# A planned attention kernel: heads paired four apart in eight q transfers, weights in 1 KB runs, a new order

## The chip, the cores and the metric

The kernel runs on one core of a Trainium2 chip. Five engines work side by side, each with its own instruction queue that it follows in order: PE (TensorE) multiplies and transposes into PSUM, DVE (VectorE) and ACT (ScalarE) copy from PSUM and compute elementwise, POOL (GpSimd) computes on SBUF, SP (SyncE) issues transfers, as ACT does in the beginning. The metric is the device time of one execution in microseconds (us), the median of several runs.

## The reference

Eight batches of 8 heads, 576 tokens, 64 channels. The first part is linear attention without a softmax, then a root-mean-square norm for each head; the second part is a mixture of four causal attention heads of which each token takes two.

```
kv  = einsum('bhsd,bhse->bhde', k, v)
out = einsum('bhsd,bhde->bhse', q, kv)
x   = out / sqrt(mean(out*out, -1) + 1e-6) * g_norm     # heads side by side: (8, 576, 512)
top-2 of x @ w_gate, softmax over the two              # gate of each token
for each of 4 experts: a = causal softmax(q k^T / 8) with q, k, v = x @ wq, wk, wv
    result += gate * (a @ v @ wo)
```

## The kernel before, in words

Tokens go in five blocks of 128 (the last has 64); the 512 channels go in four chunks of 128, a chunk being a pair of heads. Steps have short names, and the same names stand in the list that is planned:

- `lk`, `lv`, `lkr`, `lvr`, `lq` load k, v (512 tokens, then the remaining 64) and q; `lg0`, `lw`, `lwo` load the norm's weights, the gate, wq, wk, wv and wo. All go through SP, those of batch 0 half through ACT.
- `kv` multiplies k and v on PE, for each chunk two heads in the two halves of PSUM; `kvx` and `kvc` copy it; `kt`, `kg` fold the gate's weights in, so that `out` (q times kv) gives 64 channels and 4 gate values for each head.
- q must have channels on partitions. In batch 0 PE transposes it (`q`, `qc`); in the others it is loaded in 32-token pieces and DVE transposes blocks of 32 (L523).
- `oc` copies out, `sq` and `red` make the mean square, `nw` are eleven small Newton steps, `gl` to `gate` make the gates on DVE (`sh` is a subtraction, L660), `xm` scales x on POOL (L635), `x` transposes it on PE (L514), `xc` copies it.
- `v`, `qp`, `kp` project, `sc`, `exp`, `msk`, `pv` are the causal attention, `oc2`, `ot`, `y` its output, `yc` the copy of y into one of four buffers, `st` the store on SP.

The order of all instructions is written out when the program is built. `graph` lists the steps with an engine, assumed times, what each needs and which buffers it uses; `plan` walks through a model of the engines and takes the step of least `urgency` among those that can start first. The result is a fixed order on each engine; the times in those tables are the planner's assumptions. PSUM has two small buffers (`sm`) and three large ones (`bg`). DMA completions use eight semaphores in turn, so a transfer can wait for one issued eight earlier.

Of the kernel before, what the change touches and what calls it, by code (L numbers as in the profile page):

```python
# [17 lines left out]
QPE = 1  # L18
# [4 lines left out]
LOADS = ("lk", "lv", "lkr", "lvr", "lq", "lg0", "lw", "lwo", "st")  # L23


def graph(B):
    t = {}
# [16 lines left out]
    R5, R4, R2 = range(NB), range(NCH), range(EP)
    for b in range(B):

        q2 = "ACT" if b == 0 else "SP"
        for p in R4 if b == 0 else R2:
            w = 1.0 if b == 0 else 2.0
            old = [("kv", b - 2, c) for c in R4] if p == 0 else []  # L50
            add(("lk", b, p), "SP", 0.5, 0.5 * w, old, (("k", b),))
            add(("lv", b, p), q2, 0.5, 0.5 * w, old, (("v", b),))
        add(("lkr", b), "SP", 0.6, 0.7, [("kv", b - 2, c) for c in R4])
        add(("lvr", b), q2, 0.6, 0.7, [("kv", b - 2, c) for c in R4])
        for i in R5 if b < QPE else R4:
            add(("lq", b, i), q2 if i % 2 else "SP", *((0.7, 1.35 if i < NF else 0.7) if b < QPE else (2.2, 2.1)), [], (("q", b),))
        if b == 0:
            add(("lg0",), "ACT", 3.8, 0.2)
            dve(("wg",), 0.45, [("lg0",)])
            for nm in "qkv":  # L60
                for p in R2:
                    add(("lw", nm, p), "SP", 1.0, 1.5, (), (("x", nm, p),))
                    dve(("ws", nm, p), 0.48, [("lw", nm, p), ("lg0",)], (("x", nm, p),))
            for p in R2:
                add(("lwo", "o", p), "SP", 0.5, 1.5, (), (("y", "wo", p),))
                dve(("wo", "o", p), 0.42, [("lwo", "o", p)], (("y", "wo", p),))

        for c in R4:
            piece = c if b == 0 else c // 2
            pe(("kv", b, c), 0.82, [("lk", b, piece), ("lv", b, piece), ("lkr", b), ("lvr", b)], (("sm", "kv", b), ("k", b), ("v", b)))  # L70
        dve(("kvx", b), 0.84, [("kv", b, c) for c in R4] + [("out", b - 2, i) for i in R5], (("sm", "kv", b),))
        act(("kvc", b), 0.37, [("kvx", b), ("kt", b - 2)], (("sm", "kv", b),))
        for i in R5:
            if b < QPE:
                last = i == NF
                pe(("q", b, i), 0.38 if last else 0.44, [("lq", b, i)], (("sm", "q", b, i), ("q", b)))
                dve(
                    ("qc", b, i), 0.42 if last else 0.69, [("q", b, i), ("out", b - 1, i), ("out", b - 1, NF)],
                    (("sm", "q", b, i),),
                )  # L80
# [4 lines left out]
        pe(("kg", b), 0.45, [("ktc", b), ("wg",)], (("sm", "kg", b), ("kvT", b)))
        dve(("kgc", b), 0.34, [("kg", b)] + [("out", b - 2, i) for i in R5], (("sm", "kg", b),))
        for i in R5:
# [4 lines left out]
            dve(  # L92
                ("oc", b, i), 0.73, [("out", b, i), ("xm", b - 1, i), ("gl", b - 1), ("sq", b - 1, i)],
# [66 lines left out]
NF = 4  # L160
POOLS = {
# [4 lines left out]
PERIOD = 25.8  # L166
URGENCY = {
    "den": (-64.6, 21.14, -2.99), "ex": (43.8, 42.17, -5.95), "exp": (-101.9, 8.59, 2.67),
# [3 lines left out]
    "ktc": (-437.7, -29.37, 14.27), "kv": (-44.1, 6.07, 24.1), "kvc": (-223.2, 5.31, 24.45),  # L172
# [703 lines left out]
```

## Time and profile before

| | |
|---|---|
| median of 3 runs | 276.47 us (275.64 to 278.58) |
| profiled execution | 276.96 us, its span 275.2 us |
| PE busy | 229.5 us (83%) |
| DVE, ACT, POOL busy | 178.8, 157.7, 77.0 us |
| mean granted clock of PE | 0.919 |
| transfers | 40.28 MB, 146 GB/s over the span |

Busy time is a mean over stages of different kind; a stage is read from its own stretch. In a timeline row the first number is the start in us, the second the duration; in brackets stands the idle time before it and what ended it. SPq and ACTq are the issue of transfers. The granted clock is 1.00 or 0.50 at any time; means of a stretch lie between.

### The profile page before, as it was taken

The numbers are of one execution on the slowest core, as the hardware profiler recorded it, in microseconds if no ns is written. First come the engines' busy times: TensorE is split into PE (matmuls) and PEld (weight loads), VectorE is DVE, ScalarE is ACT, GpSimd is POOL, SyncE is SP. The second block draws the span as 40 slices with busy tenths as digits, with TensorE's granted clock in tenths as the row PEclk, the third lists the DMA queues.
The fourth block names the chain that finished last, engine by engine and source line by source line (L and its number), as shares of the span: only waits on it lengthen the run. The fifth ranks groups of instructions, "written<-read, shape, count | busy, mean of one in ns | idle before, by whom it ended". The sixth has DMA issues, their size and how long they took to land.

```text
span 275.2 us, 6438 instructions
## 1 busy us (share of the span) xinstructions
PE 229.5 (83%) x2423; PEld 204.3 (74%) x2436; DVE 178.8 (65%) x501; ACT 157.7 (57%) x282; POOL 77.0 (28%) x154
## 2 busy tenths in 40 slices
PE   1359387999999969995199799999499999999982
PEld 1358375999999859984179789889498989888950
DVE  0537885399889799837016855689978977712540
ACT  0020313278664837792257757369259679899773
POOL 8100061004800632360002821006601801912320
PEclk9986855699999999999569979999979999999999
DMA  7999989999589789689977931220003104005035
GB/s 233 236 163 268 220 151 262 221 168 283 85 184 271 119 192 250 114 244 226 239 156 186 227 102 23 74 79 0 2 1 136 38 2 173 2 0 175 1 136 210
DMA packets 109039, 40.28 MB, mean 146 GB/s; under 512 B 87760, under 2 KB 104144, under 8 KB 109008
## 3 DMA queue, kind: packets, MB, share of 16 engines
q1 hardware_dynamic: 104576, 38.16, 60.1%
q10 hardware_dynamic: 4432, 1.71, 2.9%
q8 instruction: 19, 0.31, 0.5%
q14 instruction: 12, 0.10, 0.1%
HBM read 30.42 MB, written 9.44 MB: 145 GB/s over the span
## 4 chain that ended last, share of the span: by engine, by line
PE 55%; DVE 15%; SPq 10%; DMA 7%; ACT 5%; issue 4%; ACTq 1%; POOL 0%; DVEq 0%; POOLq 0%
PE p_out L560 8%; PE p_sc L739 7%; PE p_v L695 7%; PE p_q L713 6%; PE p_k L713 6%; SPq L447 6%; PE p_x L514 5%; PE p_kv L496 5%; PE p_pv L773 4%; PE p_y L821 4%; DMA v_b<-in_v_dram 3%; DMA g_wide<-in_g_norm_dram 2%; DVE inv L794 2%; DMA out_dram<-y 2%; SPq L473 2%
## 5 line engine op out<-in xcount | busy, mean ns | idle before, releaser
L759 POOL TENSOR_SCALAR_AFFINE_SELECT PT<-PT 128x256 bf16<-128x256 bf16 (+1 forms) x80 | 29.7, 387 | 145.9 <-ACT PT L753 141.3
L753 ACT ACTIVATE PT<-p_sc 128x576 bf16<-128x576 f32 (+3 forms) x80 | 52.3, 717 | 7.8 <-PE p_sc L739 7.5
L635 POOL TENSOR_TENSOR x_tok<-o_sb,rs 128x512 f32<-128x512 f32 (+1 forms) x40 | 41.5, 1053 | 40.1 <-DMA q_b<-in_q_dram 29.0
L560 PE MATMUL p_out<-kvx,qT 128*128 128x136 f32 x320 | 44.7, 292 | 0.5 <-DVE osc L801 0.4
L576 ACT ACTIVATE sq<-o_sb 128x512 f32<-128x512 f32 (+1 forms) x40 | 25.4, 641 | 32.8 <-DVE o_sb L570 24.4
L560 PEld LDWEIGHTS p_out<-kvx,qT 128*128 128x128 f32 x320 | 41.8, 200 | 1.8 <-DVE osc L801 0.5
L570 DVE COPY o_sb<-p_out 128x544 f32<-128x544 f32 (+1 forms) x40 | 28.7, 717 | 20.4 <-PE p_out L560 19.1
L739 PE MATMUL p_sc<-qTp,kT 128*128 128x448 f32 (+4 forms) x192 | 38.1, 321 | 0.3 <-DVE osc L801 0.3
L582 DVE TENSOR_REDUCE ms<-sq 128x8 f32<-128x520 f32 (+1 forms) x40 | 27.0, 682 | 11.3 <-ACT sq L576 10.9
L647 ACT CAST xT<-p_x 128x512 fp32r<-128x512 f32 (+1 forms) x40 | 21.2, 556 | 17.6 <-PE p_x L514 17.2
L828 ACT COPY y<-p_y 128x512 f32<-128x512 f32 (+1 forms) x40 | 22.5, 590 | 15.2 <-DMA out_dram<-y 10.0
L739 PEld LDWEIGHTS p_sc<-qTp,kT 128*128 128x128 f32 x192 | 28.8, 194 | 3.1 <-ACT PT L753 0.8
L705 DVE CAST vext<-p_v 128x256 bf16<-128x256 f32 (+1 forms) x40 | 16.5, 418 | 21.9 <-PE p_v L695 21.1
L496 PE MATMUL p_kv<-v_b,k_b 128*64 128x64 f32 x512 | 24.8, 250 | 5.1 <-DMA v_b<-in_v_dram 4.5
L821 PE MATMUL p_y<-wo_b,OT 128*128 128x512 bf16 x67 | 20.6, 391 | 9.7 <-ACT y L828 9.1
L496 PEld LDWEIGHTS p_kv<-v_b,k_b 128*64 128x64 f32 x512 | 21.2, 161 | 9.8 <-DMA v_b<-in_v_dram 4.5
L695 PE MATMUL p_v<-wv_r,xT 128*128 128x256 f32 x160 | 27.5, 300 | 0.5 <-DVE vext L705 0.2
L514 PE MATMUL p_x<-ident_f,x_tok 128*128 128x128 f32 (+1 forms) x160 | 25.4, 292 | 2.9 <-ACT xT L647 1.3
L695 PEld LDWEIGHTS p_v<-wv_r,xT 128*128 128x128 f32 x160 | 22.6, 195 | 1.9 <-DVE vext L705 0.8
L514 PEld LDWEIGHTS p_x<-ident_f,x_tok 128*128 128x128 f32 (+1 forms) x160 | 18.6, 154 | 6.0 <-POOL x_tok L635 2.5
L728 ACT CAST kT<-p_k 64x576 fp32r<-64x576 f32 x32 | 20.3, 634 | 4.1 <-PE p_k L713 3.6
L523 DVE STREAM_TRANSPOSE qT<-q_b 128x576 f32<-128x576 f32 x28 | 20.4, 758 | 2.3 <-PE p_out L560 1.5
(74 smaller groups left out, 312.4 us busy)
## 6 DMA issues: line engine op xcount, KB each, us to landing
out_dram<-y SPq DMA_DIRECT2D x32, 256.0 KB, 2.5
q_b<-in_q_dram SPq DMA_DIRECT2D x112, 72.0 KB, 2.8
v_b<-in_v_dram SPq DMA_DIRECT2D x14, 512.0 KB, 6.2
k_b<-in_k_dram SPq DMA_DIRECT2D x14, 512.0 KB, 6.6
k_b<-in_k_dram SPq DMA_DIRECT2D x4, 256.0 KB, 5.2
v_b<-in_v_dram ACTq DMA_DIRECT2D x4, 256.0 KB, 5.3
k_rem<-in_k_dram SPq DMA_DIRECT2D x8, 128.0 KB, 7.8
out_dram<-y SPq DMA_DIRECT2D x8, 128.0 KB, 2.4
```

The source lines that it names most:

```text
L496: nc.tensor.matmul(p_kv[hh * Dh : (hh + 1) * Dh, c, :], lhsT=lhs, rhs=rhs, start=(j == 0), stop=(j == NF), skip_group_check=True,)
L514: nc.tensor.transpose(p_t[:, c, :nt], src[:nt, 2 * c : 2 * c + 2, :].rearrange("p h d -> p (h d)"), ident_f[:nt, :nt])
L560: nc.tensor.matmul(p_o[:, c // 2, (c % 2) * 2 * GW : (c % 2 + 1) * 2 * GW], lhsT=blocks_of(qT, c)[:, i * P : (i + 1) * P], rhs=kvx[b % 2][ ...
L570: nc.vector.tensor_copy(out=ob[:nt, i].rearrange("p (k h) g -> p k (h g)", k=2), in_=big("out", b, i)[:nt, :, 0 : 4 * GW])
L582: nc.vector.tensor_reduce(mss[b % 2][:nt, i, :], sqs[(NB * b + i) % 3][:nt], axis=AX_X, op=AluOpType.add)
L635: nc.gpsimd.tensor_tensor(out=buf(("x", b, i), [P, H, Dh], FP32, "x_tok")[:nt], in0=ob[:nt, i, :, 0:Dh], in1=st["rstd", b][:nt, i * H : (i ...
L695: nc.tensor.matmul(p_v[:], lhsT=blocks_of(xTs[b % 2], c)[:, i * P : (i + 1) * P], rhs=w_r["v"][:, c, :, :].rearrange("p e f -> p (e f)"), ...
L713: nc.tensor.matmul(p_p[:, s, 0:HALF], lhsT=w_r[nm][:, c, 2 * pr : 2 * pr + 2, :].rearrange("p e f -> p (e f)"), rhs=blocks_of(xTs[b % 2], ...
L739: nc.tensor.matmul(p_s[:, el, o : o + hi - lo], lhsT=kTs[pr][el][:, kb * P : (kb + 1) * P], rhs=tiles["qTp", b, pr][:, lo:hi], start=True, ...
L753: nc.scalar.activation(PT[:, :, d0 : d0 + o], big("sc", b, pr, j)[:, :, 0:o], ACTF.Exp, scale=scale)
L759: nc.gpsimd.affine_select(out=d, in_=d, compare_op=AluOpType.is_ge, fill=0.0, base=0, pattern=[[0, 2], [1, w]], channel_multiplier=-1,)
L821: nc.tensor.matmul(p_y[:], lhsT=blocks_of(OTs[b % 2], pr)[:, qc * P : (qc + 1) * P], rhs=wo_b[:, pr, :], start=(pr == 0), stop=(pr == EP - 1),
```

## The change

Four parts, and an order planned anew.

1. Heads. From batch 2 on, chunk c holds heads c and c+4 instead of 2c and 2c+1, so one q transfer takes two chunks: eight of 32x36x32 for a batch instead of sixteen of 32x18x32. Batches 0 and 1 (`QPE = 2`, it was 1) go through PE with neighbouring heads. `oc` puts the heads back in their places, and a second set of gate weights (`wg_sp`) is loaded.
2. Weights. wq, wk, wv come in six transfers, each partition taking four successive channels in one run of 1 KB, where twelve took runs of 256 bytes. Channel 4p+c is then on partition p of chunk c, so the transposes of x read channels c, c+4, c+8 ...; the norm's weight for these is a small load more (`g_rows`), and POOL multiplies it in instead of DVE.
3. Copies out of PSUM. A table names for each copy the batches in which the other engine does it.
4. Out matmuls write their four chunks at multiples of 256 in PSUM instead of closely.

The planner has new rules: steps in `PORT` wait for POOL, loads wait until at most `RING` us of transfers are ahead, PE steps before `COLD` cost 1.8 times as much, and a PE step needs what the reader of its PSUM buffer needs of earlier batches.

```diff
-QPE = 1
+QPE = 2
+ON_ACT = ("kvc", "xc", "qpc", "kpc", "otc", "yc")
+SWAP = {"kgc": (6,), "ktc": (1,), "kvc": (0,), "kvx": (1,), "oc": (0, 1), "otc": (1,), "qc": (1,), "qpc": (7,), "vc": (1, 6), "xc": (0, 6, 7), "yc": (0, 1, 6)}
+
+def engine_of(n):
+    return "ACT" if (n[0] in ON_ACT) != (n[1] in SWAP.get(n[0], ())) else "DVE"
...
+    for n, (eng, _, _, needs, tiles) in t.items():
+        for tl in tiles if eng != "PE" else ():
+            for m in makers.get(tl, ()):
+                t[m][3].extend(x for x in needs if earlier(x, m) and x not in t[m][3])
...
+LG0 = 5.0
+COLD = 15.005
+RING = 4.5
+PORT = ("nw", "gl", "sh", "mk", "gt", "gate", "iv")
-PERIOD = 25.8
+PERIOD = 173.5
 URGENCY = {
-    "den": (-64.6, 21.14, -2.99), "ex": (43.8, 42.17, -5.95), "exp": (-101.9, 8.59, 2.67),
+    "den": (51.7, -21.4, -19.57), "ex": (292.1, 19.87, -23.53), "exp": (295.6, -38.9, -16.04),
...
+                if n[0] in PORT:
+                    t = max(t, free["POOL"])
+                if n[0] in LOADS:
+                    t = max(t, dma - RING)
...
+    def head(b, c, hh):
+        return 2 * c + hh if b < QPE else NCH * hh + c
...
-        for r in range(4):
-            eng.dma_start(
-                q_t(b)[r * 32 : (r + 1) * 32, i, :, :],
-                q[b, 2 * i + r // 2, :, (r % 2) * 32 : (r % 2 + 1) * 32].rearrange("(g t) d -> t g d", t=32),
-            )
+        r, c0, n = i % 4, i // 4 * 2, 2 * (S // 32)
+        eng.dma_start(
+            q_t(b)[r * 32 : (r + 1) * 32, c0 : c0 + 2].rearrange("p c g d -> p (c g) d"),
+            q[b, head(b, c0, r // 2) : head(b, c0, r // 2) + 2, :, (r % 2) * 32 : (r % 2 + 1) * 32].rearrange(
+                "h (g t) d -> t (h g) d", t=32
+            ),
+        )
...
-        wf = buf(("x", nm, m), [P, 2, E, Hd], FP32, "w_stage")
-        for c in range(2):
-            rows = slice((2 * m + c) * P, (2 * m + c + 1) * P)
-            nc.sync.dma_start(wf[:, c, :, :], w_dram[nm][:, rows, :].rearrange("e p f -> p e f"))
+        nc.sync.dma_start(
+            buf(("x", nm, p), [P, 2, NCH * Hd], FP32, "w_stage")[:],
+            w_dram[nm][2 * p : 2 * p + 2].rearrange("e (p c) f -> p e (c f)", c=NCH),
+        )
     def ws(nm, p):
-        nc.vector.tensor_scalar_mul(
-            out=w_r[nm][:, 2 * m : 2 * m + 2].rearrange("p c e f -> p (c e f)"),
+        nc.gpsimd.tensor_tensor(
+            out=w_r[nm][:, :, 2 * p : 2 * p + 2, :].rearrange("p c e f -> p e c f"),
...
+            nc.scalar.dma_start(wg_sp[pp], by_head[:, c2 : H : 2, :])
+        nc.scalar.dma_start(
+            g_rows[:], g_norm.rearrange("(p c) -> p c", c=NCH).unsqueeze(0).to_broadcast([P * NCH // Dh, Dh // NCH, NCH])
+        )
...
     def out_mm(b, i):
-                p_o[:, c // 2, (c % 2) * 2 * GW : (c % 2 + 1) * 2 * GW],
+                p_o[:, c // 2, (c % 2) * 256 : (c % 2) * 256 + 2 * GW],
...
     def x_tr(b, i):
-        transpose_in(i, tiles["x", b, i], "x", b, i)
+        t = tiles["x", b, i][:].rearrange("p h d -> p (h d)")
+        transpose_in(i, lambda c: t[:, c : c + NCH * (P - 1) + 1 : NCH], "x", b, i)
```

The order at three places. On DVE in the beginning, before (`kT`, `xT` are set to zero, `kvx` is the copy of kv's product `p_kv`, `qT` and `kvT` follow it):

```order
L387 CAST kT_141<-zrow 64x640
L390 CAST kT_138<-zrow 128x64
L526 COPY qT<-p_q 128x4x128
L390 CAST kT_141<-zrow 128x64
L505 COPY kvx_78<-p_kv 64x4x64 x2
L526 COPY qT<-p_q 128x4x128
L536 COPY kvT<-p_kt 128x256
```

On the same engine from its first instruction, now:

```order
L456 COPY kvx_78<-p_kv 64x4x64
L399 CAST xT_108<-zrow 128x64
L399 CAST xT_112<-zrow 128x64
L433 CAST kT_132<-zrow 64x640
L433 CAST kT_135<-zrow 64x640
L436 CAST kT_132<-zrow 128x64
L433 CAST kT_138<-zrow 64x640
L436 CAST kT_135<-zrow 128x64
L433 CAST kT_141<-zrow 64x640
L436 CAST kT_138<-zrow 128x64
L456 COPY kvx_78<-p_kv 64x4x64
L436 CAST kT_141<-zrow 128x64
```

Nine of the casts stood ahead of the copy of kv and now stand between its two halves.

On ACT at the start of batch 0's norm, before (`sq` is the square of `o_sb`, which DVE has copied):

```order
L459 DMA wg_st<-in_moe_w_gate_dram 64x2x4 x4
L345 ACT_TABLE_LOAD
L345 ACTIVATE warm<-zrow 128x1
L508 COPY kvc_80<-p_kv 128x256
L576 ACTIVATE sq_94<-o_sb 128x8x64
```

The same place now:

```order
L522 DMA wg_st<-in_moe_w_gate_dram 64x2x4 x2
L391 ACT_TABLE_LOAD
L391 ACTIVATE warm<-zrow 128x1
L523 DMA wg_sp<-in_moe_w_gate_dram 64x4x4
L525 DMA g_rows<-in_g_norm_dram 128x1x4
L454 COPY o_sb<-p_out 128x544
L650 ACTIVATE sq_94<-o_sb 128x8x64
L454 COPY o_sb<-p_out 128x544 x2
L650 ACTIVATE sq_96<-o_sb 128x8x64
```

The copies of out stand between the squares, the copy of kv has gone, and two small loads come after the table load.

On SP where the first results are stored, before:

```order
L447 DMA q_b<-in_q_dram 32x18x32 x12
L832 DMA out_dram<-y 64x512
L447 DMA q_b<-in_q_dram 32x18x32 x4
L420 DMA v_b<-in_v_dram 128x4x256
L420 DMA k_b<-in_k_dram 128x4x256
L420 DMA v_b<-in_v_dram 128x4x256
L420 DMA k_b<-in_k_dram 128x4x256
L432 DMA k_rem_74<-in_k_dram 64x8x64
L432 DMA v_rem_76<-in_v_dram 64x8x64
L447 DMA q_b<-in_q_dram 32x18x32 x12
L832 DMA out_dram<-y 128x512 x5
```

And now, from the second store on:

```order
L907 DMA out_dram<-y 128x512
L508 DMA q_b<-in_q_dram 32x36x32
L907 DMA out_dram<-y 128x512 x2
L508 DMA q_b<-in_q_dram 32x36x32
L493 DMA k_rem_83<-in_k_dram 64x8x64
L493 DMA v_rem_85<-in_v_dram 64x8x64
L481 DMA k_b<-in_k_dram 128x4x256
L481 DMA v_b<-in_v_dram 128x4x256
L481 DMA k_b<-in_k_dram 128x4x256
L481 DMA v_b<-in_v_dram 128x4x256
L508 DMA q_b<-in_q_dram 32x36x32 x6
L907 DMA out_dram<-y 128x512
```

Before, one store, then 22 loads, then five stores; now four stores among single q transfers, then 13 loads.

## Rows read from the trace of the kernel before

**Rows 1.** Page, 40 equal slices of the span, busy tenths of PE and of DMA.

```profile
PE   1359387999999969995199799999499999999982
...
DMA  7999989999589789689977931220003104005035
```

**Rows 2.** Stretches: us; busy us (count) of PE, PEld, DVE, ACT, POOL; PEclk; DMA.

```profile
37.00:48.00 11.00, 8.05 (x51) 6.15 (x48) 7.05 (x23) 3.01 (x7) 5.15 (x5) 0.50 0.90 221
...
58.00:120.00 62.00, 58.64 (x716) 53.57 (x717) 52.95 (x154) 41.90 (x76) 22.99 (x37) 1.00 0.87 185
...
128.00:136.00 8.00, 0.00 (x0) 0.00 (x0) 2.47 (x4) 0.29 (x1) 0.00 (x0) 0.73 1.26 199
...
136.00:142.00 6.00, 5.30 (x41) 4.05 (x43) 1.32 (x2) 3.63 (x7) 0.00 (x0) 0.50 0.67 191
```

**Rows 3.** Timeline of the first 35 us: start, us, engine, line, operation, count.

```profile
11.21 0.48 PE L496 MATMUL p_kv<-v_rem,k_rem 128*64 128x64 f32 x4 [5.57 <-DMA v_rem<-in_v_dram]
...
11.44 1.10 PE L496 MATMUL p_kv<-v_b,k_b 128*64 128x64 f32 x16
...
12.18 5.47 ACTq L459 DMA_DIRECT2D wg_st<-in_moe_w_gate_dram  x4
...
17.68 1.28 ACT L345 ACT_TABLE_LOAD   x1 [17.68 <-DMA wg_st<-in_moe_w_gate_dram]
...
23.65 5.92 PE L560 MATMUL p_out<-kvx,qT 128*128 128x136 f32 x40
...
34.51 0.18 DVE L594 TENSOR_SCALAR half<-ms 128x40 int32<-128x40 int32 x1
```

**Rows 4.** Groups of instructions by line and shape: busy us, mean ns; idle before.

```profile
L387 DVE CAST kT<-zrow 64x640 fp32r<-64x640 f32 x4 | 3.2, 812 | 0.1
...
L390 DVE CAST kT<-zrow 128x64 fp32r<-128x64 f32 x4 | 0.7, 184 | 0.0
...
L576 ACT ACTIVATE sq<-o_sb 128x512 f32<-128x512 f32 x32 | 20.4, 643 | 26.5 <-DVE o_sb L570 18.2 <-DVE inv L790 2.4 <-DVE rd L683 1.7
...
L582 DVE TENSOR_REDUCE ms<-sq 128x8 f32<-128x520 f32 x32 | 21.6, 683 | 8.4 <-ACT sq L576 8.1
```

**Rows 5.** Timeline, PE: transposes of x cold and warm, then out matmuls.

```profile
40.64 1.12 PE L514 MATMUL p_x<-ident_f,x_tok 128*128 128x128 f32 x4
...
72.88 1.07 PE L514 MATMUL p_x<-ident_f,x_tok 128*128 128x128 f32 x8
...
73.78 1.09 PE L560 MATMUL p_out<-kvx,qT 128*128 128x136 f32 x8
```

**Rows 6.** Timeline, 122 to 137 us: SP queue, ACT, PE.

```profile
122.74 9.99 SPq L447 DMA_DIRECT2D q_b<-in_q_dram  x12
...
132.82 5.51 SPq L832 DMA_DIRECT2D out_dram<-y  x7
...
135.71 1.13 ACT L828 COPY y<-p_y 128x512 f32<-128x512 f32 x2 [10.04 <-DMA out_dram<-y]
...
136.34 1.01 PE L821 MATMUL p_y<-wo_b,OT 128*128 128x512 bf16 x2 [8.67 <-ACT y L828]
```

**Rows 7.** Timeline, 191 to 199 us; last row, the subtraction's group.

```profile
191.70 4.14 DVE L660 TENSOR_TENSOR sh<-lg,m 128x20 f32<-128x20 f32 x1
...
193.77 3.03 POOL L635 TENSOR_TENSOR x_tok<-o_sb,rs 128x512 f32<-128x512 f32 x3
...
198.70 0.62 PE L541 MATMUL p_kg<-wg_bd,kvT 128*128 128x16 f32 x4 [3.51 <-DVE kvT L536]
...
L660 DVE TENSOR_TENSOR sh<-lg,m 128x20 f32<-128x20 f32 x8 | 8.3, 1040 | 0.1
```

**Rows 8.** Groups by line and shape; second row, of x_tok: ns least, median, most.

```profile
L628 DVE TENSOR_REDUCE lg<-gl 128x20 f32<-128x160 f32 x8 | 3.5, 441 | 0.3
...
L514 PEld LDWEIGHTS p_x<-ident_f,x_tok x160: 134/141/231, 38.3 to 242.7; 128*128 128x128 f32 x128, 64*128 64x128 f32 x32
...
L560 PEld LDWEIGHTS p_out<-kvx,qT 128*128 128x128 f32 x320 | 41.8, 200 | 1.8 <-DVE osc L801 0.5 <-ACT PT L753 0.3
```

More of the change, by code (lines that the diff above doesn't have):

```diff
@@ L1 @@
+import math
 from contextlib import ExitStack
@@ L39, in dve, with copy @@
         add(name, "DVE", took - 0.05, took + 0.05, needs, tiles)
+    def copy(name, on_act, on_dve, needs, tiles=()):
+        if engine_of(name) == "ACT":
+            act(name, on_act, needs, tiles)
+        else:
+            dve(name, on_dve, needs, tiles)
     def pool(name, took, needs, tiles=()):
@@ L48, in graph @@
         for p in R4 if b == 0 else R2:
[L49 to L56, printed above, removed]
+            lat = 0.92 if b == 0 else 1.84
@@ L57, in graph @@
+            add(("lk", b, p), "SP", 0.55, lat, (), (("k", b),))
+            add(("lv", b, p), q2, 0.55, lat, (), (("v", b),))
+        add(("lkr", b), "SP", 0.65, 0.67, [("kv", b - 2, c) for c in R4])
+        add(("lvr", b), q2, 0.65, 0.67, [("kv", b - 2, c) for c in R4])
+        for i in R5 if b < QPE else range(8):
+            lat = (1.32 if i < NF else 0.66) if b < QPE else 1.06
+            add(("lq", b, i), q2 if i % 2 else "SP", 0.6, lat, (), (("q", b),))
         if b == 0:
-            add(("lg0",), "ACT", 3.8, 0.2)
@@ L72, in graph @@
-        act(("kvc", b), 0.37, [("kvx", b), ("kt", b - 2)], (("sm", "kv", b),))
+            pieces = (c,) if b == 0 else (c // 2,) if b < QPE else R2
+            nd = [(m, b, p) for m in ("lk", "lv") for p in pieces] + [("lkr", b), ("lvr", b)]
+            pe(("kv", b, c), 0.76, nd, (("sm", "kv", b), ("k", b), ("v", b)))
+        copy(("kvx", b), 0.76, 0.84, [("kv", b, c) for c in R4] + [("out", b - 2, i) for i in R5], (("sm", "kv", b),))
+        copy(("kvc", b), 0.37, 0.43, [("kvx", b), ("kt", b - 2)], (("sm", "kv", b),))
@@ L76, in graph @@
                 pe(("q", b, i), 0.38 if last else 0.44, [("lq", b, i)], (("sm", "q", b, i), ("q", b)))
-                dve(
-                    ("qc", b, i), 0.42 if last else 0.69, [("q", b, i), ("out", b - 1, i), ("out", b - 1, NF)],
+                copy(
+                    ("qc", b, i), 0.37 if last else 0.59, 0.42 if last else 0.69, [("q", b, i), ("out", b - 1, i), ("out", b - 1, NF)],
                     (("sm", "q", b, i),),
@@ L217, in plan @@
             waits.setdefault(m, []).append(n)
-    cand = {e: set() for e in ("PE", "ACT", "DVE", "POOL", "SP")}
+    engines = ("PE", "ACT", "DVE", "POOL", "SP")
+    cand, at = {e: set() for e in engines}, {n: i for i, n in enumerate(tasks)}
     for n in tasks:
@@ L398, with copy @@
     st = {}
+    def head(b, c, hh):
+        return 2 * c + hh if b < QPE else NCH * hh + c
+    def copy(kind, b, dst, src):
+        if engine_of((kind, b)) == "ACT":
+            nc.scalar.copy(dst, src)
+        else:
+            nc.vector.tensor_copy(out=dst, in_=src)
     def queue(b, second):
@@ L525, in q_copy @@
         nt = blocks[i][1]
-        nc.vector.tensor_copy(out=tokens(qT, i), in_=small(None, "q", b, i)[:, :, :nt])
+        copy("qc", b, tokens(qT, i), small(None, "q", b, i)[:, :, :nt])
     def kt(b):
@@ L535, in kt_copy @@
     def kt_copy(b):
-        nc.vector.tensor_copy(out=buf(("kvT", b), [P, EP, P], FP32, "kvT")[:], in_=small(None, "kt", b)[:])
+        copy("ktc", b, buf(("kvT", b), [P, EP, P], FP32, "kvT")[:], small(None, "kt", b)[:])
     def kg(b):
@@ L704, in v_copy @@
         nt = blocks[i][1]
-        nc.vector.tensor_copy(
-            out=vexts[b % 2][:nt, i, :, 0:Hd], in_=small(None, "v", b, i)[:nt].rearrange("p (e f) -> p e f", e=E)
+        copy(
+            "vc", b, vexts[b % 2][:nt, i, :, 0:Hd], small(None, "v", b, i)[:nt].rearrange("p (e f) -> p e f", e=E)
         )
@@ L815, in ot_copy @@
     def ot_copy(b, pr):
[L816 removed]
+        copy("otc", b, OTs[b % 2][:, pr * S : (pr + 1) * S], small(None, "ot", b, pr)[:, 0:S])
     def y_mm(b, qc):
```

159 lines of the change are left out of this document (88 added, 71 removed), and 40 rows, old and new, of tables (EDGES, URGENCY).

## The prediction

> **What bounds the kernel now.** I read the slices of the page first, then the stretches, then the timeline of each stretch in which TensorE (PE) is not full. In the slices the row to see is PE's: uneven for the first seven slices, 9 nearly everywhere after, with deep dips at the 19th, 20th and 29th slice, and a low end. The DMA row is mostly at 7 to 9 up to the 24th slice and at 5 or less after it [rows 1]. So transfers limit at most the beginning, and PE sets the pace from then on. The stretches say how well: from 58 to 120 us PE is busy 58.64 of 62 us at full clock. Two other stretches are bad: 37 to 48 us, where the granted clock is 0.50, and 128 to 136 us, where PE does nothing at all, after which it runs 136 to 142 us at 0.50 [rows 2].
>
> The beginning, up to 58 us, is a chain, not a throughput: the first matmuls of k and v stand until the last 64 tokens (the remainders) have landed (11.21 us), the first out matmul starts at 23.65, the Newton steps at 34.51 [rows 3], and each block of x is transposed on PE at half clock, 1.12 us for four where 0.45 is the full-clock price (eight begin at 72.88 and the next group at 73.78, so 0.90 for eight) [rows 5].
>
> The hole at 128 us is the SP queue's. It issues 12 transfers of q in 9.99 us, and seven stores stand behind them until 132.82; ACT's copy of y waits for a store (10.04 us), because the four y buffers are used up, and PE's y matmuls wait for that copy [rows 6]. A third stall is VectorE's (DVE): one subtraction of 128x20 takes 4.14 us, while GpSimd runs x_tok back to back (three more begin at 193.77), and PE then waits 3.51 us for a copy behind it [rows 7].
>
> **The change, term by term**, against the profiled execution's 275.2 us of span.
>
> *Start to the first out matmul.* Remainders now load first, so the matmuls of the first batch follow their own pieces; the last piece lands when all the bytes have, near 11.2, and its 16 records take 1.10 us at that clock [rows 3]: done near 12.7, some microseconds sooner than now, when all four groups complete only after 11.21. Against that, the DVE order now has nine setup casts between the two halves of the copy of kv: four at 812 ns, three at 184, two of the size of the latter, 4.2 us [rows 4]. Before, they filled idle time. The copy kvc goes to DVE, so it no longer waits for ACT's table load, which ends at 18.96 [rows 3]: a gain as well. Roughly even on this path. The other path is ACT's queue: four gate loads occupied it until 17.65; now there are six with a table load (1.28) ahead of the last, so the gate weights come some 1.4 to 2 us later. This path ends last. I take **+1.0**, bounds -1.0 and +2.5.
>
> *Copies and squares of the first batch.* From the first out matmul to the Newton steps now takes 10.9 us (23.65 to 34.51), DVE doing copies, reductions and five weight scalings. The copies go to ACT. No row has that copy on ACT; squares of nearly that size take 643 ns, so ten operations are 6.4, then one reduction of 683 [rows 4], behind a first out block of about 2 (five take 5.92 with the waits between them [rows 3]): 9.1, and some 0.3 for hand-overs. **-1.5**, bounds -2.5 and +0.5. All six scalings move to GpSimd, which has nothing else in that time, at about 1 us each, the price of x_tok (3.03 for three [rows 7]); they need the small load of g, at about 22 us, so they end near 29: cost nothing while the Newton steps end after that, and would cost up to 3 us if that load came 5 us later than I think.
>
> *x of the first batch.* The same matmuls in nearly the same order at the same half clock, with DVE making the copies instead of ACT: **0**, bounds -3 and +2.
>
> *q of batch 1 on PE.* Five groups of transposes are new: one cold (1.1) and four near 0.45 [rows 5], **+2.8**, all of it on PE's path; all cold it would be 5.5. The four DVE stream transposes that go away were beside other work, so they give nothing.
>
> *The hole at 128.* Eight larger transfers replace sixteen, and the order places the stores of the first y between them, the longest run of loads in front of a store being seven of q and six of k and v. Four stores have been issued before that run, so while it lasts one y waits and three buffers can still be filled. So 8.0 us of idle PE [rows 2] and half of the 5.30 busy at 0.50 come back: **-10.6**. Bounds: -12 if what waited behind them moves up too, -1 if another queue of loads stands before a store.
>
> *The port waits.* The eight subtractions take 8.3 us of DVE, 1040 ns each [rows 7], half of it in the one of 4.14, the only one seen to stop PE. The new order puts the subtraction later in most batches, but in batch 5 it still stands at the start of x_tok. **-2.0**, bounds -6 and +3 (a longer wait elsewhere).
>
> *Fewer, larger packets* (weights in 1 KB runs, q of batch 1 in 256-byte runs): the DMA row is at 9 up to slice 24 without PE waiting, apart from the beginning and the remainders [rows 1]. **0**, below zero by 1 where a load is first used, in the terms above. If PE caught up with the loads this would be worth more, not less.
>
> *Copies swapped between ACT and DVE, gaps in PSUM of the out matmuls.* By the table in the diff 35 copies go to DVE and 28 to ACT, and ten other operations leave DVE, the fuller of the two (52.95 of 62 us [rows 2]). **0**, bounds -3 and +3.
>
> *x transposes with weights four elements apart.* Each of the 160 loads now takes one 4-byte element of every 16 bytes. No row has such a load on PE. The floor is nothing: the transposes come every 112 ns [rows 5] with loads of 141 ns at the median, and eight out matmuls with loads of 200 pass in 1.09 us, the latency of the last included [rows 5, 8], so a load may show some 55 ns more before it paces PE. The nearest row for the other end is DVE's reduction lg<-gl, which reads 160 elements 16 bytes apart in 441 ns; the reduction of 520 contiguous elements takes 683 [rows 4, 8]. If the contiguous one runs at one element per 1.04 ns (an estimate), it has 142 ns fixed, and the other then takes 1.87 ns for each of its 160. A load of 128 with 0.83 ns more for each shows 106 ns more, 50 beyond the cover: 160 times, 8 us. If it occupies PE for the full 240 ns in place of 112, it is 20 us. I take **0**: the cover is real in rows of the same engine, the slower reading only in another's.
>
> The Trainium skill (SBUF — State Buffer, Door 1: The DMA port swizzle, the note on cachelines) says that SBUF lines are 16 bytes and that every access that crosses to a new line pays; by it these loads would slow, and if by as much as DVE's reads the sum would be 8 to 20 us higher. The DVE row agrees with it; no run so far shows it for PE.
>
> Sum: 1.0 - 1.5 + 2.8 - 10.6 - 2.0 = -10.3, a span of 264.9. The profiled execution took 276.96 with 1.76 around the span, 0.5 over the median of the runs shown (276.47). So 264.9 + 1.76 - 0.5 = **266 us**.
>
> **The rivals.**
> 1. *A store still stands behind loads.* The SP queue stays in order and now has stores waiting for y in front of loads as well. For it: the row of 9.99 us shows how long a run of q transfers takes, and each transfer is twice as large. Against: the buffers counted above. It decides if a store's data are ready 4 us or more before the queue reaches it while the fourth buffer is needed. The 10.6 stay lost: 276.6.
> 2. *Slower weight loads in the x transposes.* One mechanism on the one engine that is full: the transposes of x, from the point where a load shows more than about 200 ns; at 64 ns more for each transpose it has eaten the whole gain (10.3 us over 160). For it the DVE row, against it the cover that the out matmuls show. By the two ends above: 274 to 286; likeliest of these 282, slower.
> 3. *The new order packs PE better.* The whole table of urgencies is another, and the order now counts the GpSimd port and the cold clock. If the dip at 180 to 204 goes wholly (3.51 idle [rows 7] and the slow clock after it), the port waits give 6, and the end gains 3, it is 255.
>
> **Chances.** Forecast (258 to 272) 0.47; store rival 0.17; slow loads 0.20, of which 0.12 slower than before; better packing 0.16. The range that holds 8 in 10: **253 to 281**, which leaves out the slow loads near full price and the far end of the packing. A difference of 1% (so 273.7 to 279.2 is the same) is about what a measurement of this kernel can tell. Faster: 0.46 + 0.05 + 0.02 + 0.16 = 0.69. Same: 0.01 + 0.11 + 0.06 = 0.18. Slower: 0.01 + 0.12 = 0.13.
>
> **What would show it.** Right: PE busy between 100 and 150 us without a hole of more than 2 us, no wait of ACT's y copy for a store; the first out matmul at 23 to 26 us; nine casts on DVE between the halves of the kv copy; the Newton steps of batch 0 beginning near 34; the transposes of x still some 112 ns apart at full clock. Wrong: loads of x_tok over 200 ns and transposes 160 ns or more apart (rival 2); a store issued at the end of a run of q transfers while PE idles (rival 1); a beginning that ends later than 60 us, because the gate weights or the scaled weights come late, which would take back the start's terms and several microseconds more.

## The result, and the profile after

The changed kernel takes 259.56 us (median of 4 runs, 258.6 to 260.15) beside 276.36 for the kernel before: ratio 0.938, 95% interval 0.932 to 0.944. Measured again later, it took 259.64 (258.8 to 262.5) beside 277.97. The forecast was 266 us, faster; it is faster by 16.8 us in place of 10.3. Ratios here are formed from undisturbed runs alone, so one need not equal the quotient of two medians.

The page of the changed kernel, slices of the span, for PE, its granted clock and DMA:

```profile
PE   0726928999999999999999999989999999999963
PEclk9977775589999999999999999999999999999995
...
DMA  6998999999999379999898594131120202123045
```

Against [rows 1] PE's row has nothing below 8 from the seventh slice to the last two, and after the ninth slice the clock is not lost again until the last. DMA is as full as before, up to nearly the same microsecond (the slice in which it falls off begins at 155, before at 158): the loads have not become shorter, PE stands still less while they run. The stretches of [rows 2], in the changed kernel:

```profile
37.00:48.00 11.00, 8.53 (x66) 6.87 (x66) 5.11 (x19) 1.70 (x5) 5.09 (x5) 0.50 1.07 269
58.00:120.00 62.00, 61.70 (x745) 57.77 (x744) 49.20 (x141) 41.80 (x77) 17.68 (x32) 1.00 0.94 199
128.00:136.00 8.00, 7.60 (x75) 7.20 (x72) 6.12 (x17) 4.58 (x11) 2.59 (x3) 1.00 1.09 129
136.00:142.00 6.00, 6.00 (x52) 6.00 (x51) 5.53 (x15) 2.43 (x5) 0.00 (x0) 1.00 0.89 277
```

The hole at 128 is full of work and the stretch behind it at full clock; the 3.4 us of idle time from 58 to 120 became 0.3; the slow x phase of the first batch is as it was. PE is busy for as long as before (228.5 us, it was 229.5), so nearly all of the gain is idle time. After 50 us three gaps of the kernel before, other than the hole, are gone, and two of them are not in the rows of the prediction. The timeline of the kernel before, around these two, and the group of `gt` there:

```profile
95.73 3.03 POOL L635 TENSOR_TENSOR x_tok<-o_sb,rs 128x512 f32<-128x512 f32 x3
95.79 2.02 DVE L675 TENSOR_TENSOR gt<-ex,mk 128x20 f32<-128x20 f32 x1
...
99.44 0.70 PE L773 MATMUL p_pv<-vext,PT 128*128 128x65 bf16 x18 [2.74 <-DVE osc L801]
...
155.85 2.61 DVE L794 TENSOR_TENSOR inv<-inv,gate 128x6 f32<-128x6 f32 x1
...
156.05 2.03 POOL L635 TENSOR_TENSOR x_tok<-o_sb,rs 128x512 f32<-128x512 f32 x2
...
158.62 0.82 PE L773 MATMUL p_pv<-vext,PT 128*128 128x65 bf16 x18 [1.74 <-DVE inv L790]
...
L675 DVE TENSOR_TENSOR gt<-ex,mk 128x20 f32<-128x20 f32 x8 | 4.2, 528 | 1.0 <-ACT ex L666 0.9
```

They look like the one of [rows 7]: a tiny DVE operation that takes 2 to 4 us while GpSimd (POOL) multiplies x_tok, and PE waiting behind it. The releaser named in the first is osc, which was not slow itself: gt, ahead of it on DVE, was. The prediction calls these port waits; b_xsmall below tests the cause. In the changed kernel the same operations, by line and shape (sh had 1040 ns, gt 528):

```profile
L735 DVE TENSOR_TENSOR sh<-lg,m 128x20 f32<-128x20 f32 x8 | 2.3, 292 | 0.1
...
L750 DVE TENSOR_TENSOR gt<-ex,mk 128x20 f32<-128x20 f32 x8 | 1.4, 174 | 0.2
```

Not every such wait is gone: three `inv` of 128x4 that begin during an x_tok take 0.75 to 0.96 us. But after 50 us PE has no gap of 0.9 us or more left.

### The profile page after: what moved, and what is told of

The parts are those of the page before. It is cut to its first block, busy times and chain, and to the rows that moved or that the text cites. A ratio compares the mean times of both kernels' runs of the same rounds, so it can differ in the third digit from the quotient of the medians.

```text
span 257.8 us, 6403 instructions
## 1 busy us (share of the span) xinstructions
PE 228.5 (89%) x2456; PEld 205.5 (80%) x2456; DVE 169.7 (66%) x503; ACT 152.5 (59%) x277; POOL 82.6 (32%) x160
## 4 chain that ended last, share of the span: by engine, by line
PE 78%; DMA 7%; DVE 6%; ACT 4%; SPq 1%; issue 1%; POOL 0%; DVEq 0%; POOLq 0%; ACTq 0%
PE p_out L630 15%; PE p_sc L814 9%; PE p_x L585 8%; PE p_q L788 7%; PE p_kv L567 7%; PE p_y L896 7%; PE p_v L770 7%; PE p_k L788 7%; PE p_pv L848 5%; DMA q_b<-in_q_dram 3%; DMA k_b<-in_k_dram 3%; ACT PT L828 2%; PE p_ot L886 2%; DMA w_stage<-in_moe_wv_dram 2%; PE p_kg L611 1%
## 5 line engine op out<-in xcount | busy, mean ns | idle before, releaser
L828 ACT ACTIVATE PT<-p_sc 128x512 bf16<-128x512 f32 (+3 forms) x80 | 50.6, 718 | 3.4 <-PE p_sc L814 3.0
L814 PE MATMUL p_sc<-qTp,kT 128*128 128x288 f32 (+4 forms) x192 | 39.0, 323 | 0.0
L585 PE MATMUL p_x<-ident_f,x_tok 128*128 128x128 f32 (+1 forms) x160 | 28.3, 307 | 5.2 <-POOL x_tok L709 4.1
L456 DVE COPY o_sb<-p_out 128x544 f32<-128x544 f32 (+1 forms) x30 | 21.4, 716 | 11.2 <-PE p_out L630 11.0
L585 PEld LDWEIGHTS p_x<-ident_f,x_tok 128*128 128x128 f32 (+1 forms) x160 | 23.1, 209 | 7.1 <-POOL x_tok L709 5.5
L896 PE MATMUL p_y<-wo_b,OT 128*128 128x512 bf16 x80 | 23.8, 400 | 1.0 <-ACT OT L454 0.7
L788 PE MATMUL p_q<-xT,wq_r 128*128 128x288 f32 x128 | 21.9, 323 | 0.0
L454 ACT CAST xT<-p_x 128x512 fp32r<-128x512 f32 (+1 forms) x25 | 13.3, 545 | 14.3 <-PE p_x L585 14.2
L788 PE MATMUL p_k<-xT,wk_r 128*128 128x288 f32 x128 | 20.2, 303 | 0.0
L788 PEld LDWEIGHTS p_q<-xT,wq_r 128*128 128x128 f32 x128 | 19.3, 206 | 0.3
## 6 DMA issues: line engine op xcount, KB each, us to landing
out_dram<-y SPq DMA_DIRECT2D x32, 256.0 KB, 2.0
q_b<-in_q_dram SPq DMA_DIRECT2D x6, 256.0 KB, 7.5
v_b<-in_v_dram ACTq DMA_DIRECT2D x4, 256.0 KB, 5.3
k_b<-in_k_dram SPq DMA_DIRECT2D x4, 256.0 KB, 6.7
```

The costliest lines, as they stand in the source:

```text
L454: nc.scalar.copy(dst, src)
L585: nc.tensor.transpose(p_t[:, c, :nt], chunk(c)[:nt], ident_f[:nt, :nt])
L788: nc.tensor.matmul(p_p[:, s, 0:HALF], lhsT=w_r[nm][:, c, 2 * pr : 2 * pr + 2, :].rearrange("p e f -> p (e f)"), rhs=blocks_of(xTs[b % 2], ...
L814: nc.tensor.matmul(p_s[:, el, o : o + hi - lo], lhsT=kTs[pr][el][:, kb * P : (kb + 1) * P], rhs=tiles["qTp", b, pr][:, lo:hi], start=True, ...
L828: nc.scalar.activation(PT[:, :, d0 : d0 + o], big("sc", b, pr, j)[:, :, 0:o], ACTF.Exp, scale=scale)
L896: nc.tensor.matmul(p_y[:], lhsT=blocks_of(OTs[b % 2], pr)[:, qc * P : (qc + 1) * P], rhs=wo_b[:, pr, :], start=(pr == 0), stop=(pr == EP - 1),
```

## The experiments

**GpSimd's work cut, in the kernel before** (b_xsmall).

```diff
+        hs = H if b == 0 else 1
         nc.gpsimd.tensor_tensor(
-            out=buf(("x", b, i), [P, H, Dh], FP32, "x_tok")[:nt],
-            in0=ob[:nt, i, :, 0:Dh],
-            in1=st["rstd", b][:nt, i * H : (i + 1) * H].unsqueeze(2).to_broadcast([nt, H, Dh]),
+            out=buf(("x", b, i), [P, H, Dh], FP32, "x_tok")[:nt, 0:hs],
+            in0=ob[:nt, i, 0:hs, 0:Dh],
+            in1=st["rstd", b][:nt, i * H : i * H + hs].unsqueeze(2).to_broadcast([nt, hs, Dh]),
...
```

> The kernel before with GpSimd's x_tok multiplication cut to one head of eight in every batch but the first (the rest of x_tok keeps older numbers, so this part of the computation is left out); the order of all engines stays. GpSimd then runs about 0.2 us per block in place of 1.05, so that DVE operations with two SBUF operands have nothing to wait for. Theory A (all three PE gaps of before at 96.7, 156.9 and 195.2 us, 2.74 + 1.74 + 3.51 = 8.0 us, are port waits behind x_tok, and the half clock after two of them costs 3 more): sh, gt and inv below 0.4 us each, these three gaps gone, 276.4 - 8 to 11 = 265 to 268 us; the hole at 128 stays. Theory B (the prediction's: only the 4.14 us subtraction stopped PE, the other two gaps are DVE being late for other reasons): one gap gone, the others stay, 272 to 274.5 us.

268.0 us (267.7 to 269.6), ratio 0.972 (0.967 to 0.977): 8.4 us gained, theory A. Its groups, and PE's longest waits (us in total, times, longest):

```profile
L661 DVE TENSOR_TENSOR sh<-lg,m 128x20 f32<-128x20 f32 x8 | 2.6, 328 | 0.1
...
L676 DVE TENSOR_TENSOR gt<-ex,mk 128x20 f32<-128x20 f32 x8 | 1.5, 184 | 1.0 <-ACT ex L667 0.9
```

```profile
PE p_y L822 <- ACT y L829: 13.4, 3, 13.0
PE p_kv L496 <- DMA v_rem<-in_v_dram: 5.3, 1, 5.3
```

All three gaps are gone. The hole grew from 8.7 to 13.0 us: PE came to it 3 us earlier and the stores were no sooner free. So 8.4 is what is left of the port waits after the hole took back the 3 us gained before it. The edit also gives x to PE earlier; that alone could be worth little, since PE waited 1.2 us for x_tok in the whole of the kernel before. That DVE waits for GpSimd's instructions is read from the durations, here and at the start of a_again below; no run changes the port alone.

**The stores, in the kernel before** (b_stores).

```diff
+        order = [n for _, _, n in plan(tasks, POOLS, {n: urgency(n) for n in tasks})[0]]
+        late = [("lq", 6, 1), ("lq", 6, 2), ("lq", 6, 3)]
+        order = [n for n in order if n not in late]
+        at = order.index(("st", 0, 0)) + 1
+        order[at:at] = late
```

> The kernel before with one thing moved: the twelve q transfers of batch 6 that stood between the first stores of y and the next ones are issued after the four stores of the first batch; all else in the old order. Theory of the prediction (the hole at 128 us is the SP queue's alone and is worth 10.6 us): no PE gap above 1 us between 120 and 142 us, clock at full there, 276.4 - 10.6 = 265.8 us (264 to 268). Rival (something else stands right behind it, the loads that now come later or another store): less than 4 us, 272 or more, with a PE gap a few us further on.

273.1 us, of four runs of 269.0, 271.6, 274.7 and 275.4: too wide for a ratio, and the median lies in the rival's range while the quickest run does not. The gap at 128 is gone, and 1.9 us remain at 138.5, behind ACT's copy of y. The profiled execution (271.6) tells the stretch of the hole apart from the rest. An out matmul in front of the hole and the first matmul of kv behind it, before:

```profile
114.58 1.09 PE L560 MATMUL p_out<-kvx,qT 128*128 128x136 f32 x8
...
139.21 1.12 PE L496 MATMUL p_kv<-v_b,k_b 128*64 128x64 f32 x16
```

And with the loads moved:

```profile
118.34 1.09 PE L560 MATMUL p_out<-kvx,qT 128*128 128x136 f32 x8
...
132.86 0.69 PE L496 MATMUL p_kv<-v_b,k_b 128*64 128x64 f32 x16
```

This stretch is 10.1 us shorter, close to the 10.6 of the prediction. The 3.8 us by which PE came to it later were lost before 124.4 us, where the SP queue first differs in order, so they are not the edit's: PE was 4.5 us ahead at the kv of batch 2 and then met q late:

```profile
83.21 0.78 DVE L523 STREAM_TRANSPOSE qT<-q_b 128x576 f32<-128x576 f32 x1 [3.40 <-DMA q_b<-in_q_dram]
...
84.35 1.12 PE L695 MATMUL p_v<-wv_r,xT 128*128 128x256 f32 x4 [2.67 <-DVE vext L705]
```

**Both, with the stores at three places** (b_both, b_both2, b_both3). x_tok cut as above; the loads of batch 6 in three orders on SP's queue (`st(0,*)` are the stores of batch 0, a bar parts what follows one another).

```
 b_both:  st(0,*) | last 12 of q(6) | st(1,3) st(1,4) st(1,2)
 b_both2: st(0,*) | 4 of q, k, v, rem, 12 of q(6) | st(1,3) st(1,4) st(1,2)
 b_both3: st(0,*) | k, v, rem(6) | st(1,3) st(1,4) st(1,2) | q(6)
```

> Both edits on the kernel before: the q transfers of batch 6 behind the four stores, and x_tok cut to one head of eight from the second batch on (that part is left out). Theory A (store hole and port waits together are where the time went): the two gains add, 276.4 - 19 to 22 = 254.5 to 257.5 us, which is below the changed kernel by about what its added work costs. Theory B (store hole 10.6 and one port wait 2 to 3.5, the rest of the change's gain from better packing of the order): 262 to 264 us.

> The kernel before with x_tok cut to one head of eight from the second batch on (that part is left out), and now all loads of batch 6 (four of k and v, the two remainders, sixteen of q) issued after the stores of the first batch, not only the last twelve of q. Theory A (hole and port waits are the whole of the time that went; 263.2 us were left with the stores half moved because 5.75 + 1.51 us of PE gap at 124 and 138 us, and the half clock after them, were still there): these gaps fall below 1 us in all, 253.5 to 256.5 us; the changed kernel is then slower than this by its added work alone. Theory B (the loads are the bound there: what is issued later lands later): the gap moves to a wait for k, v or q of batch 6, 260 us or more.

> The kernel before with x_tok cut to one head of eight from the second batch on (left out), and the loads of batch 6 placed between the stores: k, v and remainders after the stores of the first batch, q after the first three stores of the second. Theory A (stores must stand between loads: moving the loads behind one group of stores only moved the hole to the next group, 11.2 us at 131): no PE gap above 1.5 us between 100 and 160, 253.5 to 257 us. Theory B (the loads themselves are late at that place): a gap of 5 us or more remains, 262 or more.

263.2 us (ratio 0.954, 0.948 to 0.960), 267.3 (0.968, 0.962 to 0.973) and 259.6 (0.937, 0.929 to 0.944). The first two missed theory A and lie in the ranges of theory B, but not for its reasons: in b_both all three port waits were gone and PE waited 5.75 and 1.51 us for ACT's copy of y; in b_both2 the gap did not move to a wait for the loads of batch 6. In the second the first stores were early and the hole stood one group further on, 11.2 us of PE behind ACT's copy of y, with its stores behind the loads:

```profile
117.75 3.11 SPq L833 DMA_DIRECT2D out_dram<-y  x2
120.96 2.08 SPq L447 DMA_DIRECT2D q_b<-in_q_dram  x4
...
128.96 9.89 SPq L447 DMA_DIRECT2D q_b<-in_q_dram  x12
138.95 1.69 SPq L833 DMA_DIRECT2D out_dram<-y  x3
```

The third, with stores between two groups of loads:

```profile
117.21 4.78 SPq L833 DMA_DIRECT2D out_dram<-y  x5
122.08 0.39 SPq L420 DMA_DIRECT2D k_b<-in_k_dram  x1
...
126.88 3.31 SPq L833 DMA_DIRECT2D out_dram<-y  x3
130.28 17.89 SPq L447 DMA_DIRECT2D q_b<-in_q_dram  x28
```

PE still waits for ACT's copy of y in two places, 2.0 us at 132 and 1.6 at 163, and the time is 2.6 above the end of what was expected, between the two theories. It equals the changed kernel's 259.64, measured beside the same runs of the kernel before. Two mechanisms taken out of the kernel before are worth as much there as the whole change (18.3 us), though with GpSimd's work left out. What the change adds (below) it must save elsewhere; the swapped copies are one such place.

**The changed kernel again** (a_again), as the measure for its edits.

> The changed kernel unchanged, as the measure for the edits of it: in three of them the gate weights were ready 3.5 us later than in its profile (PE's wait for wg_bd 3.5 in place of 1.3 us, first out matmul at 29 in place of 25.1). Theory A (the start differs from run to run and chip to chip, and PE makes up for part of it at a better clock): its own runs spread over 258 to 261 with a first out matmul anywhere from 25 to 29 us. Theory B (the start is fixed and the edits moved it): 259.6 within 0.7, first out matmul at 25.

259.64 us (258.8 to 262.5), theory A: the spread of the runs is as expected. Its profiled execution, the slowest of the six, begins the out matmuls at 28.1 us, not at 25.1, and shows why. DVE's scaling of the gate weights, beside GpSimd's of the projections:

```profile
23.47 2.04 POOL L546 TENSOR_TENSOR wq_r<-w_stage,g_rows 128x512 fp32r<-128x512 f32 x2 [15.42 <-DMA g_rows<-in_g_norm_dram]
23.65 0.89 DVE L532 TENSOR_SCALAR wg_bd<-wg_st,g_wide 64x16 f32<-64x16 f32 x1
24.45 1.08 DVE L533 TENSOR_SCALAR wg_bd<-wg_sp,g_wide 64x16 f32<-64x16 f32 x1
...
25.57 0.97 DVE L532 TENSOR_SCALAR wg_bd<-wg_st,g_wide 64x16 f32<-64x16 f32 x1
26.45 1.08 DVE L533 TENSOR_SCALAR wg_bd<-wg_sp,g_wide 64x16 f32<-64x16 f32 x1
...
28.14 6.91 PE L630 MATMUL p_out<-kvx,qT 128*128 128x136 f32 x40 [0.45 <-DVE kvx L456]
```

And in the first profile of the same kernel, where GpSimd began a microsecond after DVE was done:

```profile
23.26 0.21 DVE L532 TENSOR_SCALAR wg_bd<-wg_st,g_wide 64x16 f32<-64x16 f32 x1
23.40 0.22 DVE L533 TENSOR_SCALAR wg_bd<-wg_sp,g_wide 64x16 f32<-64x16 f32 x1
...
25.07 6.57 PE L630 MATMUL p_out<-kvx,qT 128*128 128x136 f32 x40 [0.45 <-DVE kvx L456]
```

The port wait once more, at the start, and which of the two is first differs from run to run. The late start is the commoner one in the profiles: in a_contig and a_noqt, which leave this part of the start as it is, the out matmuls begin at 29.0 and 29.1 us. The 3 us are partly made up: at the kv of batch 2 this execution is 3.2 behind the other, at the end of PE's work 2.4.

**The x transposes** (a_contig: contiguous reads alone, which leaves the channel order wrong; a_wold: the weights' part of the change undone as well, twelve transfers in 256-byte runs, still scaled on GpSimd). The edit that both have:

```diff
-        transpose_in(i, lambda c: t[:, c : c + NCH * (P - 1) + 1 : NCH], "x", b, i)
+        transpose_in(i, lambda c: t[:, c * P : (c + 1) * P], "x", b, i)
```

> The changed kernel with the x transposes reading 128 contiguous channels of x_tok instead of every fourth (x then no longer meets its own weight rows: the channel order is left wrong, the amount of work is the same). Theory A (the strided weight load paces PE by some 11 ns a transpose, 121 in place of 109 to 112 ns, 160 times): loads back from 210 to about 140 ns, step to 110 ns, 259.6 - 1.8 = 257.8 us (257 to 258.5). Theory B (hidden, since PE waits for other things around these transposes): step falls but the time stays at 259.6 within 0.5 us.

> The changed kernel with the weights' part undone: twelve transfers in 256-byte runs with the channels in their own order, scaled by g of the partition, and contiguous x transposes; all else as it is. Theory A (contiguous transposes gain about 2 us, as in the run with them alone, and the smaller packets of the weights cost under 1): 257 to 258.3. Theory B (the 256-byte runs load the first 30 us, in which the queues are full): 259.5 or more, first out matmul or the x phase later by 2 us.

256.0 us (0.924, 0.918 to 0.929) and 255.6 (0.923, 0.917 to 0.929): 3.6 and 4.0 us less than the changed kernel, about twice what was expected. Groups of the transposes, the changed kernel first, then a_wold (mean ns after the comma):

```profile
L585 PEld LDWEIGHTS p_x<-ident_f,x_tok 128*128 128x128 f32 x128 | 18.6, 209 | 6.2 <-POOL x_tok L709 5.5 <-issue 0.4
L585 PE MATMUL p_x<-ident_f,x_tok 64*128 64x64 f32 x32 | 5.5, 297 | 0.2 <-DVE xT L456 0.2
```

```profile
L585 PEld LDWEIGHTS p_x<-ident_f,x_tok 128*128 128x128 f32 x128 | 15.3, 149 | 7.4 <-POOL x_tok L709 6.6 <-issue 0.4
...
L585 PE MATMUL p_x<-ident_f,x_tok 64*128 64x64 f32 x32 | 3.6, 234 | 0.4 <-DVE xT L456 0.4
```

From start to start (medians at full clock) the transposes of 128 tokens went from 109 to 121 ns and those of the last 64 tokens from 63 to 120. So 128 x 12 + 32 x 57 ns = 3.4 us. The profiled executions share the gain out in another way. From the kv of batch 2 to the end of PE's work a_contig takes 2.6 us less than a_again (190.6 and 193.2), where seven of the eight batches give 2.9 by this sum. The rest came before, where the granted clock differed too (1.00 beside 0.69 from 50 to 60 us), and that part is not shown to be the transposes' own. The packets of the weights cost nothing that these runs can tell: a_wold has 4700 packets more than the changed kernel and is as fast as a_contig.

**q of batch 1 without PE** (a_noqt).

```diff
     def q_tr(b, i):
+        if b == 1:
+            return
...
+        if b == 1:
+            src = q_t(b)[:, min(i, 3)].rearrange("p (c a) d -> p c (a d)", a=2)[:, :, :nt]
+            return copy("qc", b, tokens(qT, i), src)
```

> The changed kernel without the PE transposes of q of batch 1: the copies to qT read the loaded q itself (batch 1 then works on q that is not transposed, block 3 used in place of block 4). Theory A (the prediction's term: all of their time is on PE's path): 259.6 - 2.8 = 256.8 us (256 to 257.5). Theory B (PE stands there anyway behind the Newton steps and the x phase of batch 0, or the loads, so that the groups fill idle or half-clock time): 258.8 to 260.

259.9 us (257.7 to 261.3; 0.941, 0.935 to 0.946): no gain that can be told, theory B by the time. In its profile the kv of batch 2 begins at 61.1, 1.8 us before that of a_again, whose out matmuls began a microsecond earlier, and PE ends 1.2 earlier; the runs do not show it. What takes the rest back stays open.

**The copies on their usual engines** (a_noswap), the order kept.

```diff
-        if engine_of((kind, b)) == "ACT":
+        if kind in ON_ACT:
```

> The changed kernel with each PSUM copy on its usual engine (no exceptions by batch), the order kept. Theory A (the prediction's: at the start the copies on ACT are worth 1.5 us, elsewhere the swaps cost or give nothing): 260.5 to 262. Theory B (the swaps are what keeps DVE ahead of PE in the edge batches): 264 us or more, with PE gaps behind DVE copies. Theory C (they change nothing): 259 to 260.2.

267.1 us (266.4 to 268.3; 0.968, 0.964 to 0.973): 7.5 us slower than a_again, theory B by the time. The PE gaps behind DVE's copies that it named did not come: PE waits longer than in a_again for ACT's kvc at the start (4.8 us; 3.4 there, for DVE's qT), for the first x_tok (6.2; 5.2) and for copies of y on ACT (2.0 in all; 0.4). Of the 6.0 us between the two profiled executions at the end of PE's work, 1.2 are there at the kv of batch 2 and 3.1 at that of batch 7; what follows adds the other 2.9. The last 40 us of PE's work, a_again and then a_noswap (busy us of PE, PEld, DVE, ACT, POOL):

```profile
216.00:256.00 40.00, 37.73 (x360) 32.38 (x362) 24.86 (x78) 30.39 (x55) 12.28 (x25) 1.00 0.24 84
```

```profile
222.00:262.00 40.00, 36.46 (x343) 30.19 (x342) 16.33 (x67) 33.13 (x60) 12.36 (x25) 1.00 0.22 77
```

Without the swaps ACT carries more and DVE a third less, and PE gets less done. The order was made for the swaps, so 7.5 us is what they are worth in it, not what they would give the kernel before.

**The start** (a_gate, a_best2). In a_gate the setup casts come first on DVE, and ACT issues the gate loads right after k and v. a_best2 has in addition the four gate scalings ahead of the q copies, and the weights' part undone.

```diff
+    ctx.enter_context(tc.manual_schedule())
...
-    nc.scalar.activation(warm[:], zrow[:, 0:1], ACTF.Exp)
...
-        eng = queue(b, i % 2)
+        eng = nc.sync
...
+        nc.scalar.activation(warm[:], zrow[:, 0:1], ACTF.Exp)
...
+    order.remove(("wg",))
+    order.insert(order.index(("ktc", 0)) + 1, ("wg",))
```

The first line makes the written order hold from the setup casts on; `warm`, which brings the table load, moves behind the gate loads; the last two lines are a_best2's alone.

> The changed kernel with its start in another order: the nine setup casts first on DVE, ACT's queue issues the six gate loads right after k and v (its two q loads go to SP) and loads its table after them. Theory A (the first out matmul at 25.1 us is set by the gate weights, which land at 23.3): first out matmul near 20, 3 to 5 us gained, 254.5 to 256.5. Theory B (the loads set the start: k and v of batch 1 land at 32.7 us whatever the gate weights do, and PE runs the time before at half clock): gain under 1 us, 258.6 to 260.

> The changed kernel with three edits: setup casts first on DVE, gate loads right after k and v on ACT's queue, the four gate scalings right after the copy of kvT on DVE (they stood behind all q copies and beside GpSimd's weight scalings, where they took 1 us each in place of 0.2), and the weights' part undone as above. Theory A (start set by the gate weights): first out matmul near 21, x phase 3 us earlier, 253 to 255.5. Theory B (loads set it): 256.5 to 258.5, p_x waits for k and v of batch 1.

a_gate: 258.1 us, with runs from 253.3 to 259.3: by its median between the theories, and too wide to say more. Its profiled execution took 258.2, and there the gate weights were ready, but the scalings stood behind the q copies, at 20.5, beside GpSimd again, three of the four taking 1 us; the out matmuls began at 24.3. a_best2: **250.6 us** (248.9 to 252.5; ratio 0.906, 0.900 to 0.911), faster than was expected and than both kernels, 9.0 below the changed one and 5.0 below a_wold, which has the same weights and the old start. Its timeline:

```profile
16.83 0.23 DVE L534 TENSOR_SCALAR wg_bd<-wg_sp,g_wide 64x16 f32<-64x16 f32 x1
...
21.51 7.17 PE L631 MATMUL p_out<-kvx,qT 128*128 128x136 f32 x40 [0.45 <-DVE kvx L456]
...
33.17 1.12 PE L568 MATMUL p_kv<-v_b,k_b 128*64 128x64 f32 x16 [4.49 <-DMA v_b<-in_v_dram]
...
35.51 0.90 PE L586 MATMUL p_x<-ident_f,x_tok 128*128 128x128 f32 x3
```

Out matmuls 5.8 us sooner than in a_wold (27.3), the x phase 4.9 sooner; now k and v of batch 1 are what PE waits for.

## Why the prediction was right in direction and short in size

- **Port waits, -2.0 [-6, +3]: the step that failed.** The prediction took the 4.14 us subtraction as the only one that stops PE, and priced it at 2.0. Two more gaps (2.74 and 1.74 us) had the same cause, though the waits name fast operations as their releasers: osc was late because gt, ahead of it on DVE, had taken 2 us. Cutting GpSimd's work gave 8.4 us, beyond the far bound, and all three gaps went. The Trainium skill (SBUF — State Buffer, Who interferes with whom) says that a DVE operation with two SBUF inputs and a GpSimd operation that reads SBUF exclude each other for the whole instruction; b_xsmall agrees, 1040 to 328 ns for the subtraction.
- **The hole, -10.6 [-12, -1]: right in place, cause and, by one profile, size.** In the changed kernel the 8.7 us of idle PE and the half clock behind them are gone. With the loads moved behind the stores and nothing else changed, the stretch around the hole was 10.1 us shorter in the profiled execution of b_stores. The median of its runs gained only 3.3, and they lie too far apart to tell; the profile shows 3.8 us lost before the edit can act. With the port waits out, the hole was worth 8.4 (268.0 to 259.6, two measurements). The rival of a store behind loads did not come in the changed kernel and did in b_both2: where stores stand between the loads decided.
- **Strided transposes, 0 with 8 to 20 at the other end: too small, 3.4 to 4.0 us by step and by time.** A load takes 69 ns more (210 to 141, medians), not the 106 worked out from DVE's row. The cover of 55 ns was nearly right for 128 tokens (12 ns show). For the last block all but 12 of the 69 ns show: there a step took 63 ns and takes 120, and the prediction counted all 160 alike. So rival 2 was true as a mechanism and smaller in price. The Trainium skill's note on lines of 16 bytes (SBUF — State Buffer, Door 1) agrees with the slower load; it gives no price for one.
- **Copies swapped, 0 [-3, +3]: too small.** The prediction set counts of copies (35 to DVE, 28 to ACT; the traces have 35 and 30) against DVE's share from 58 to 120. Only 16 of the 65 lie in that stretch, since the swaps belong to the first two and the last two batches. Taken out of the new order they cost 7.5.
- **Start +1.0, copies of batch 0 -1.5, x of batch 0 nothing: as forecast in the first profile, the start by luck.** First out matmul at 25.07 (+1.4), from there to the Newton steps 9.3 us (it was 10.9), first x transposes at 38.2 (38.3). That the start has a second outcome, 28.1 us and later, it did not see; that one is +4.5, beyond the bound of +2.5, and the port wait makes up most of the difference.
- **q of batch 1 on PE, +2.8: not seen in the runs.** Its groups take 3.2 us of PE, but leaving them out gave nothing that can be measured.
- **Packets, 0: right** for the weights, by a_wold beside a_contig. (DMA's row in [rows 1] falls off in the 24th slice, not after it; nothing hangs on that.)

The terms do not add up one by one: the swaps' 7.5 are measured inside the new order, and the port waits feed the hole. That 259.56 still lies inside the forecast's own 258 to 272, at its lower edge, is in part luck: the port waits gave more than was forecast, and the x transposes took some of it back. The rival of 255 us, with the dip at 180 to 204 and the port waits gone, told more of what happened; it put the dip down to the packing, where it was the port as well.

## What to carry to other kernels

Where several gaps of the critical engine follow a short operation that takes ten times its usual time, look at what the neighbouring engine does in that moment before taking each gap for a lateness of its own; price the whole group. A store queue that is shared with loads needs its stores spread between them, each near the moment its data are ready; moving a run of loads can move the hole. And a cover read from the wide instructions of a kind does not hold for its narrow ones.

## What the runs showed of the hardware that was not expected

- A DVE operation that waits for GpSimd can wait past several GpSimd instructions: the subtraction of [rows 7] stood from 191.70 to 195.84 while GpSimd ran an x_tok, three masks of bf16 and two more x_tok without a pause. An operation that scales a single SBUF tensor by one value for each partition waits too: the gate scalings, 0.22 us alone, took 0.89 to 1.08 beside GpSimd.
- A TensorE weight load of 128 fp32 columns 16 bytes apart took 210 ns (median) beside 141 when they are contiguous, and for 64 rows 213 beside 138.
